# One table of 785 steps in another order, and two small PSUM banks named apart

## The chip, the cores and the metric

The kernel runs on one core of one Trainium2 chip. The metric is the device time of one launch in microseconds. The kernel before takes 190.54 us in the median of three runs (190.48, 190.54 and 190.9).

## What is computed

Attention with a window of 96 keys and 8 global keys, for 4 batches of 8 heads (768 tokens, 64 features a head), followed by a mixture of experts in which every expert reads 4 slots that are softmax mixtures of all tokens:

```python
def _attn_ref(q, k, v, n_global, n_local):
    scores = scale * np.matmul(q, k.transpose(0, 1, 3, 2))
    ...
    scores = np.where(keep, scores + bias, -1000000000.0)
    ...
    a = np.exp(scores - np.max(scores, axis=-1, keepdims=True))
    a = a / (np.sum(a, axis=-1, keepdims=True) + 1e-09)
    return np.matmul(a, v)

def _moe_ref(x, phi, w1, w2):
    logits = x @ phi                      # 3072 tokens, 32 slots
    ...
    slot_input = d.T @ x                  # d: softmax over the tokens
    ...
    slot_out[e] = np.maximum(slot_input[e] @ w1[e], 0.0) @ w2[e]   # 8 experts, hidden size 1024
    ...
    return c @ slot_out                   # c: softmax over the slots
```

## The kernel before

**Attention units.** The work of attention is cut into 16 units u (a batch and a pair of heads). For each unit, TensorE makes the scores in three parts (`scores`, L601) into two PSUM buffers. DVE adds the bias table and keeps a running maximum (`biased`, L610, three a unit). TensorE turns the maximum (`max_t`, L617), DVE reduces it (`max_n`, L622). ACT takes the exponential of each head i (`exponential`, L627) and rounds it to f16 (`w_hi`, L630). What the rounding leaves is made in three parts for each head, on POOL (`w_lo`) or on DVE (`w_lo_dve`), both recorded under L637. The values are split in the same way: the high half on ACT (`v_hi_act`, L575) or on POOL (`v_hi`, L572), the low half on DVE (`v_lo`, L579). TensorE multiplies 39 small tiles a head (`values`, L655; the last unit goes in halves, `valh`, L708). DVE then takes the sums, their reciprocals and the product out of PSUM (`ev_sums` L667, `ev_recs` L672, `ev_mul` L676). The product is turned (`tr`, L738) and copied (`tr_copy` on ACT, L744; `tr_copy_dve` on DVE, L749), and makes the logits (`logits`, L770). At the end of each batch (units 3, 7, 11, 15) follow `logits_all` (L787), `strip_max`, `strip_exp` (L811), `by_token` (L826), its copies, `dispatch` (L849) and `dispatch_sum` (L860, L866); `strip_sum` (L819, L821) adds up a denominator that is read only near the end.

**Experts.** Behind unit 15 the steps `ld_...` finish the slot inputs, `hid` (L115) is the first matrix product of the experts, `proj` (L149) the second, in two halves of the columns; `so` (L208, L209) scales a half, `cmb` (L1094) mixes it back to tokens, `cev` on ACT (L1100) and `cev_dve` on DVE (L1103) copy it out of PSUM, and `put` (L1107) sends 0.52 MB of output, 12 times. `check` (L1121 to L1132) and `flag` (L1137) decide whether a general path must run instead.

**Loads.** All loads are issued by SP, one after the other: `load_qk` (L457, 0.85 MB a unit, two buffers `raw0` and `raw1`), `load_v` (L460, 0.46 MB a unit, two halves of `vt`), and the weights (L438), 32 pieces of 1.05 MB. Pieces 0 to 9 have tiles of their own (`wp0` to `wp9`) and are loaded during attention (`piece`); `extra` loads parts of later pieces into space that attention leaves unused. `free` loads the rest of such a piece as soon as a buffer of attention is done, and `load` loads pieces 23 to 31, most of them over pieces that `hid` has used. An instruction of SP that waits holds back all that stand behind it.

**The order.** Everything stands in one list, `ORDER`, that is walked once (`for name, u, *args in ORDER: steps[name](u, *args)`). Each step appends its instructions to their engines, and each engine runs its own in that order. No scheduler moves anything later. Each of the steps of TensorE that needs a small PSUM bank takes one from `Banks.tile`; during attention there are two such banks, both under the tag `m` of a pool with two buffers.

## Time and profile before

| what | value |
|---|---|
| median of three runs | 190.54 us |
| span of the profiled execution (no other time is given for it) | 190.8 us |
| busy: PE, DVE, ACT, POOL | 170.4, 144.1, 127.0, 96.9 us |
| moved by DMA | 61.34 MB, mean 321 GB/s |
| first `biased`, end of the last `w_lo_dve` | 7.98 us, 126.6 us |
| first `hid`, last copy of `cmb` | 136.30 us, 181.0 us |

Busy shares are averages over the two very different stretches, attention up to some 128 us and the experts behind it. The page's chain of waits is empty for this execution, so its path has to be read from the waits of each engine, from the timeline and from tables of short stretches.

### The profile page before, as it was taken

To read this page: it belongs to the slowest core of one execution; us is meant where nothing else is said; L and a number is where in the kernel's file an instruction comes from. 1 tells how busy PE (TensorE), PEld (TensorE's weight loads), DVE (VectorE), ACT (ScalarE), POOL (GpSimd) and SP (SyncE) were. 2 spreads that over 40 slices of the span, in tenths; PEclk is the share of its full clock that TensorE was granted. 3 is DMA by queue.
4 is the path that set the end of the run, shared out by engine and by line. 5 is a ranking of instruction groups with operands and counts; after the bars stand their busy time and mean duration, and the time that the engine had idled before them with its cause. 6 is when DMAs were issued, how large, how long until landed. Compare 5 with 4: busy or idle time off the path is not lost.

```text
span 190.8 us, 6334 instructions
## 1 busy us (share of the span) xinstructions
PE 170.4 (89%) x2629; PEld 127.6 (67%) x2629; DVE 144.1 (75%) x353; ACT 127.0 (67%) x165; POOL 96.9 (51%) x121
## 2 busy tenths in 40 slices
PE   8898999999997988899999999897999999998600
PEld 2454988889895787689878887784622566875400
DVE  4899999999988999879999999996850413535600
ACT  3068799899999598698999999964204352632600
POOL 7506687788679776679696897500004040000000
PEclk9999999999999999999999999999999999999975
DMA  3998999989999999619519977899999999977992
GB/s 108 411 405 294 339 411 414 386 344 364 367 406 401 380 332 356 228 32 334 174 41 352 336 267 225 279 413 349 364 423 425 404 417 410 399 258 265 324 330 89
DMA packets 18609, 61.34 MB, mean 321 GB/s; under 512 B 1680, under 2 KB 8976, under 8 KB 16144
## 3 DMA queue, kind: packets, MB, share of 16 engines
q1 hardware_dynamic: 18432, 60.89, 85.4%
q8 instruction: 22, 0.36, 0.7%
q14 instruction: 11, 0.09, 0.1%
q10 hardware_dynamic: 144, 0.00, 0.0%
HBM read 54.59 MB, written 6.29 MB: 319 GB/s over the span
## 4 chain that ended last, share of the span: by engine, by line


## 5 line engine op out<-in xcount | busy, mean ns | idle before, releaser
L637 POOL TENSOR_TENSOR ph<-tb,ph 128x432 f16<-128x432 f32 x79 | 82.3, 1074 | 23.5 <-ACT ph L630 23.5
L601 PE MATMUL sc<-raw 64*128 64x216 f32 (+2 forms) x448 | 44.9, 337 | 3.1 <-DMA raw<-in_qk_dram 2.0
L627 ACT ACTIVATE tb<-tb,nb 128x1296 f32<-128x1296 f32 x32 | 43.7, 1374 | 2.0 <-DVE nb L622 1.9
L630 ACT CAST ph<-tb 128x1296 f16<-128x1296 f32 x32 | 40.6, 1272 | 5.2 <-PE x L655 4.6
L601 PEld LDWEIGHTS sc<-raw 64*128 64x128 f32 x448 | 37.0, 186 | 10.2 <-issue 3.3
L655 PEld LDWEIGHTS <-ph 128*128 128x128 f16 x1170 | 38.8, 97 | 2.9 <-issue 2.1
L655 PE MATMUL x<-v,ph 128*128 128x65 f16 (+1 forms) x1170 | 40.4, 193 | 0.0
L579 DVE SCALAR_TENSOR_TENSOR v<-vt,v 128x896 f16<-128x896 f32 x16 | 19.8, 1237 | 1.0 <-POOL v L572 1.0
L186 POOL TENSOR_TENSOR wp<-lnat,wp 120x448 f32<-120x448 f32 x4 | 4.5, 1150 | 29.0 <-ACT wp L181 29.0
L610 DVE CUSTOM_DVE_ANT_1 tb<-sc,tt,mx 128x864 f32<-128x864 f32 x16 | 17.7, 1108 | 0.7 <-DVE tt L296 0.2
L738 PE MATMUL m<-ident,xn 120*128 120x120 f32 x112 | 16.7, 275 | 1.4 <-DVE xmax L676 1.2
L575 ACT ACTIVATE v<-vt 128x896 f16<-128x896 f32 x12 | 11.4, 949 | 7.9 <-DMA vt<-in_v_dram 7.9
L676 DVE CUSTOM_DVE_ANT_1 xn<-x,rc 120x896 f32<-120x896 f32 x15 | 16.3, 1087 | 0.4
L738 PEld LDWEIGHTS m<-ident,xn 120*128 120x128 f32 x112 | 11.5, 141 | 4.1 <-issue 2.8
L637 DVE TENSOR_TENSOR ph<-tb,ph 128x432 f16<-128x432 f32 x17 | 11.4, 690 | 0.0
L115 PE MATMUL hp<-wp,sl 128*32 128x512 f32 x80 | 10.5, 593 | 0.0
L1100 ACT COPY xta<-m 128x512 f32<-128x512 f32 x7 | 4.0, 587 | 8.6 <-PE m L1094 8.5
L610 DVE CUSTOM_DVE_ANT_1 tb<-sc,xta,mx 128x864 f32<-128x864 f32 x8 | 8.9, 1112 | 0.5 <-DVE mx L610 0.2
L610 DVE CUSTOM_DVE_ANT_1 tb<-sc,xtt,mx 128x864 f32<-128x864 f32 x8 | 8.9, 1116 | 0.4 <-DVE mx L610 0.4
L610 DVE CUSTOM_DVE_ANT_1 tb<-sc,tt 128x864 f32<-128x864 f32 x8 | 8.4, 1050 | 0.2
L1103 DVE COPY tt<-m 128x512 f32<-128x512 f32 x5 | 3.4, 690 | 6.4 <-PE m L1094 6.4
L149 PE MATMUL o<-wp,wp 128*32 128x256 f32 x96 | 7.6, 380 | 0.0
(206 smaller groups left out, 283.6 us busy)
## 6 DMA issues: line engine op xcount, KB each, us to landing
wp<-in_w_dram SPq DMA_DIRECT2D x14, 1024.0 KB, 10.1
raw<-in_qk_dram SPq DMA_DIRECT2D x15, 832.0 KB, 6.7
vt<-in_v_dram SPq DMA_DIRECT2D x16, 448.0 KB, 6.7
wp<-in_w_dram SPq DMA_DIRECT2D x4, 512.0 KB, 12.7
raw<-in_w_dram SPq DMA_DIRECT2D x4, 512.0 KB, 13.7
out_dram<-xtt SPq DMA_DIRECT2D x4, 512.0 KB, 3.3
out_dram<-xta SPq DMA_DIRECT2D x4, 512.0 KB, 6.6
out_dram<-tt SPq DMA_DIRECT2D x4, 512.0 KB, 5.7
```

What stands on the lines that cost most here:

```text
L115: nc.tensor.matmul(out=hp[n][32 * s:32 * s + 32, :], lhsT=slv(a, c, s), rhs=w1(e, c // 2)[:, (c % 2) * DF + 512 * n:(c % 2) * DF + 512 * n ...
L149: nc.tensor.matmul(out=o[32 * s:32 * s + 32, 0:w], lhsT=ht[:, c, 32 * s:32 * s + 32], rhs=w2(4 * a + s, half)[:, c0 + c * w:c0 + c * w + w ...
L575: nc.scalar.activation(out=vhi[u % 2][:, :, :, 0:D], in_=vraw[u % 2], func=AF.Copy, scale=V_SC)
L579: nc.vector.scalar_tensor_tensor(out=vlo[k].rearrange("p j i d -> p (j i) d"), in0=vraw[k].rearrange("p j i d -> p (j i) d"), scalar=V_SC, ...
L601: nc.tensor.matmul(out=z[:, i, at:at + n], lhsT=r_[r, KCOL[j]:KCOL[j] + KR], rhs=r_[r, KW + KB * j:KW + KB * j + n], start=True, stop=True)
L610: nc.vector.tensor_tensor_reduce(out=tb(u)[:, :, BW * k:BW * k + BW], in0=sc[(3 * u + k) % 2][:, :, 0:BW], in1=table.unit(u % NP, k), scal ...
L627: nc.scalar.activation(out=t, in_=t, func=AF.Exp, bias=nbs[u], scale=T_SC)
L630: nc.scalar.copy(out=blocks(phi_[i])[:, :, 0:QW], in_=tb(u)[:, i].rearrange("p (s c) -> p s c", c=QW))
L637: (engine or nc.gpsimd).tensor_tensor(out=blocks(plo_[i])[:, c, 0:QW], in0=tb(u)[:, i].rearrange("p (s c) -> p s c", c=QW)[:, c], in1=bloc ...
L655: nc.tensor.matmul(out=xf[:, at(t, i):at(t, i) + d], lhsT=w[:, c:c + P], rhs=vv[:, j, i, 0:d], start=z in first, stop=(z == len(ops) - 1), ...
L676: nc.vector.tensor_tensor_reduce(out=xnb[(u // 2) % 3][:, p].rearrange("p t (i d) -> p (t i) d", i=2), in0=xv[:, :, 0:D], in1=rcs.pop(u).u ...
L738: nc.tensor.transpose(out=m[:, at:at + KB], in_=xnb[(u // 2) % 3][:, p % 2, t, :], identity=ident[0:KB, 0:KB])
```

## The change

The list holds the same 785 steps, each as often as before, with the same arguments; they stand in another order from the first step to the last. The steps that go to DVE and those that go to POOL stay the same, so no instruction is added or removed. As the pieces of weights take their places by the order of `free`, some pieces of the experts lie in other tiles (piece 11 in `tb1` and no longer in `raw1`, for example). The two small banks, so far two buffers of one tag, become two tags `m0` and `m1`, which are taken in turn.

```diff
-ORDER = [('load_qk0', 0), ('hint', 0, 'Pool'), ('keys', 0), ('extra', 0), ('scores', 0, 0), ('load_qk', 0), ('table_even', 0),
+ORDER = [('keys', 0), ('table_even', 0), ('load_v', 0), ('warm', 0, 1), ('load_qk0', 0), ('load_qk', 0), ('scores', 0, 0),
...
-    psm = banks.enter_context(tc.tile_pool(name="psm", bufs=2, space=PSUM))
+    psm = banks.enter_context(tc.tile_pool(name="psm", bufs=1, space=PSUM))
...
-        tags = ("m", "m")
+        tags = ("m0", "m1")
...
-            return (psm if tag == "m" else self.pool).tile([P, 512], F32, name=name, tag=tag)
+            return (psm if tag[0] == "m" else self.pool).tile([P, 512], F32, name=name, tag=tag)
...
-            left.next(("l2", "l3", "m", "m", "l0", "l1"))
+            left.next(("l2", "l3", "m0", "m1", "l0", "l1"))
```

**Place 1: SP, the loads of units 6 to 11.** `vt` is the load of a unit's values, `raw0` and `raw1` those of an even and an odd unit's queries and keys, `wp5` to `wp8` pieces of weights. Before, from the loads of values 7 and 6 to those of unit 11's queries:

```order
L460 DMA vt_102<-in_v_dram 128x896 x2
L438 DMA wp6_86<-in_w1_dram 128x2048
L457 DMA raw1_91<-in_qk_dram 128x1664
L438 DMA wp7_87<-in_w1_dram 128x2048
L460 DMA vt_102<-in_v_dram 128x896
L438 DMA wp8_88<-in_w1_dram 128x2048
L457 DMA raw0_90<-in_qk_dram 128x1664
L460 DMA vt_102<-in_v_dram 128x896
L457 DMA raw1_91<-in_qk_dram 128x1664
```

Now, from the piece ahead of values 6 to unit 11's queries:

```order
L438 DMA wp5_85<-in_w1_dram 128x2048
L460 DMA vt_102<-in_v_dram 128x896
L457 DMA raw1_91<-in_qk_dram 128x1664
L460 DMA vt_102<-in_v_dram 128x896
L438 DMA wp7_87<-in_w1_dram 128x2048
L457 DMA raw0_90<-in_qk_dram 128x1664
L460 DMA vt_102<-in_v_dram 128x896 x2
L457 DMA raw1_91<-in_qk_dram 128x1664
```

Ahead of unit 10's queries (the last `raw0` of both lists) nine pieces stood in the whole queue, and six do now (9, 8, 0, 1, 5 and 7, in that order); pieces 2, 4, 6 and 3 follow later. Values 6 stand ahead of values 7.

**Place 2: DVE, unit 5's sums.** `rsall` is `ev_sums`, `v` is `v_lo` of unit 6, `ph` is a `w_lo_dve`, `state` (L819) is `strip_sum` of the first batch. Before, from the first `biased` of unit 8 to `ev_mul` of unit 5:

```order
L610 ISA tb_98,mx<-sc_172,tt 128x2x432
L610 ISA mx 128x1
L667 TENSOR_TENSOR rsall<-x,eps 120x14
L579 SCALAR_TENSOR_TENSOR v_101<-vt,v_101 128x896
L672 RECIPROCAL rc<-rsall 120x2x7
L622 ISA mxd,nb<-m,shift 128x128
L622 ISA nb 128x1
L819 COPY state<-al 128x1
L676 ISA xn_106,xmax<-x,rc 120x896
```

Now, the same stretch:

```order
L610 ISA tb_98,mx<-sc_172,tt 128x2x432
L610 ISA mx 128x1
L804 TENSOR_SCALAR state<-al 128x1
L622 ISA mxd,nb<-m,shift 128x128
L622 ISA nb 128x1
L610 ISA tb_98,mx<-sc_173,tt,mx 128x2x432
L610 ISA mx 128x1
L637 TENSOR_TENSOR ph_99<-tb_96,ph_99 128x2x216
L667 TENSOR_TENSOR rsall<-x,eps 120x14
L672 RECIPROCAL rc<-rsall 120x2x7
L579 SCALAR_TENSOR_TENSOR v_101<-vt,v_101 128x896
L676 ISA xn_106,xmax<-x,rc 120x896
```

A `biased`, a `max_n` and a `w_lo_dve` now stand ahead of the sums and of `v_lo`; `strip_sum` is gone from here and stands two units later, behind the reciprocals of unit 7.

**Place 3: DVE, the end.** `so` is the second half's scaling, `fl` is `check`, `flag` the decision, L1103 the copies of `cmb`. Before:

```order
L1131 TENSOR_REDUCE fl<-fl 128x1
L1132 TENSOR_SCALAR fl<-fl 128x1
L208 TENSOR_SCALAR so<-o,sgz 128x256
L209 SCALAR_TENSOR_TENSOR so<-o,sgz,so 128x256
L1103 COPY tt<-m 128x512
L1103 COPY xtt<-m 128x512
L1103 COPY xta<-m 128x512
L1137 TENSOR_SCALAR flag<-m 1x1
L1103 COPY tt<-m 128x512 x2
```

Now:

```order
L1103 COPY v_101<-m 128x512 x2
L208 TENSOR_SCALAR so<-o,sgz 128x256
L209 SCALAR_TENSOR_TENSOR so<-o,sgz,so 128x256
L1121 TENSOR_REDUCE fl<-fl 120x1
L1122 TENSOR_SCALAR fl<-fl 120x1
L1121 TENSOR_REDUCE fl<-rsall 120x1
L1122 TENSOR_SCALAR fl<-fl 120x1
L1121 TENSOR_REDUCE fl<-rsall 48x1
L1122 TENSOR_SCALAR fl<-fl 48x1
```

The check stood ahead of `so` and stands behind it now, ahead of DVE's five last copies.

## Rows read from the trace of the kernel before

**Rows 1.** The page: busy time by engine, and DMA's busy tenths in 40 slices.
```profile
PE 170.4 (89%) x2629; PEld 127.6 (67%) x2629; DVE 144.1 (75%) x353; ACT 127.0 (67%) x165; POOL 96.9 (51%) x121
...
DMA  3998999989999999619519977899999999977992
```

**Rows 2.** Table of stretches, 56 to 88 us: us, busy of PE, PEld, DVE, ACT, POOL, clock, DMA share, GB/s.
```profile
56.00:64.00 8.00, 6.84 (x123) 5.42 (x121) 6.62 (x15) 5.91 (x9) 7.03 (x7) 1.00 0.98 389
64.00:72.00 8.00, 7.23 (x123) 6.36 (x123) 7.82 (x18) 7.38 (x8) 5.57 (x5) 1.00 0.94 360
72.00:80.00 8.00, 6.70 (x122) 5.54 (x121) 7.67 (x17) 5.41 (x9) 6.11 (x6) 1.00 0.86 320
80.00:88.00 8.00, 8.00 (x153) 7.17 (x151) 6.21 (x13) 7.98 (x9) 5.93 (x6) 1.00 0.35 106
```

**Rows 3.** DVE's groups, 7.9 to 126.7 us: busy us, mean ns, idle ahead and releaser.
```profile
L579 DVE SCALAR_TENSOR_TENSOR v<-vt,v 128x896 f16<-128x896 f32 x16 | 19.8, 1237 | 1.0 <-POOL v L572 1.0
...
L637 DVE TENSOR_TENSOR ph<-tb,ph 128x432 f16<-128x432 f32 x17 | 11.4, 690 | 0.0
...
L667 DVE TENSOR_TENSOR rsall<-x,eps 120x14 f32<-120x14 f32 x15 | 2.5, 168 | 2.4 <-PE x L655 2.4
```

**Rows 4.** Waits of the whole span: who waited for whom, us in total, times, longest.
```profile
DVE rsall L667 <- PE x L655: 2.4, 4, 1.6
...
PE sc L601 <- DMA raw<-in_qk_dram: 2.0, 2, 1.3
...
PE m L849 <- DVE state L819: 1.2, 1, 1.2
```

**Rows 5.** Timeline of SP, POOL, DVE and PE: start us, us, instruction, idle ahead.
```profile
49.33 0.80 SPq L460 DMA_DIRECT2D vt<-in_v_dram  x2
...
56.99 0.94 POOL L572 TENSOR_SCALAR v<-vt 128x896 f16<-128x896 f32 x1 [0.96 <-DMA vt<-in_v_dram]
...
57.97 1.89 DVE L579 SCALAR_TENSOR_TENSOR v<-vt,v 128x896 f16<-128x896 f32 x1 [1.00 <-POOL v L572]
...
82.02 0.17 DVE L667 TENSOR_TENSOR rsall<-x,eps 120x14 f32<-120x14 f32 x1 [1.58 <-PE x L655]
...
77.22 1.00 PE L601 MATMUL sc<-raw 64*128 64x216 f32 x8 [1.30 <-DMA raw<-in_qk_dram]
```

**Rows 6.** Single lines and tiles: durations in ns, min/median/max.
```profile
L579 DVE SCALAR_TENSOR_TENSOR v<-vt,v x16: 1078/1086/1933, 15.0 to 121.3; 128x896 f16<-128x896 f32 x16
...
L637 DVE TENSOR_TENSOR ph<-tb,ph x17: 596/606/1010, 28.5 to 126.0; 128x432 f16<-128x432 f32 x17
...
L637 POOL TENSOR_TENSOR ph<-tb,ph x79: 997/1012/1861, 15.9 to 122.4; 128x432 f16<-128x432 f32 x79
```

**Rows 7.** Table of stretches again, at attention's end and in the experts' part.
```profile
112.00:116.00 4.00, 3.71 (x72) 3.07 (x70) 3.95 (x11) 4.00 (x8) 3.92 (x5) 1.00 0.67 183
...
140.00:144.00 4.00, 4.00 (x40) 1.17 (x36) 1.09 (x5) 0.61 (x2) 0.00 (x0) 1.00 1.01 428
...
171.00:172.00 1.00, 1.00 (x24) 0.62 (x20) 0.90 (x6) 0.26 (x1) 0.00 (x0) 1.00 0.11 39
...
186.00:187.00 1.00, 0.00 (x0) 0.00 (x0) 0.00 (x0) 0.00 (x0) 0.00 (x0) 0.50 1.00 333
```

**Rows 8.** Timeline: first `biased`, last run of `w_lo_dve`, first `hid`, `check`, last `put`.
```profile
7.98 1.06 DVE L610 CUSTOM_DVE_ANT_1 tb<-sc,tt 128x864 f32<-128x864 f32 x1
...
123.84 2.77 DVE L637 TENSOR_TENSOR ph<-tb,ph 128x432 f16<-128x432 f32 x5
...
136.30 0.62 PE L115 MATMUL hp<-wp,sl 128*32 128x512 f32 x2
...
171.44 0.15 DVE L1121 TENSOR_REDUCE fl<-fl 120x1 f32<-120x2 f32 x1
...
173.24 0.15 DVE L1132 TENSOR_SCALAR fl<-fl 128x1 f32<-128x1 f32 x1
...
181.78 1.28 SPq L1107 DMA_DIRECT2D out_dram<-tt  x1
```

More of the change, by code (lines that the diff above doesn't have):

```diff
@@ L485, in blocks @@
         return w[:, 0:6 * PB].rearrange("p (s c) -> p s c", c=PB)
-    wp = psm.tile([P, 512], F32, name="wp", tag="m")
+    wp = psm.tile([P, 512], F32, name="wp", tag="m0")
     busy_in = nc.const_aps.tensor(1.0, [P, 512], BF16)
@@ L567, in pair_of_banks @@
             return [left.wide.tile([P, 512], F32, name="hp", tag=f"y{n}") for n in range(2)]
-        left.next(("l2", "l3", "m", "m"))
+        left.next(("l2", "l3", "m0", "m1"))
         return [left.pool.tile([P, 512], F32, name="hp", tag=f"l{n}") for n in range(2)]
```

2 lines of the change are left out of this document (1 added, 1 removed).

## The prediction, made blind

> **What bounds the kernel now.** The page comes first [rows 1]: PE is busy for 170.4 us, DVE for 144.1, but these are averages over two stretches. DMA's tenths show 9 nearly everywhere, a valley in slices 16 to 20 (76 to 100 us), and 9 again from slice 26 (124 us) nearly up to the end. So I read the two stretches apart.
>
> In attention I look for the engine that never rests. DVE's groups between 7.9 and 126.7 us [rows 3] show only a few microseconds of idle time, most of it in two places: the sums out of PSUM waited 2.4 us for `values` in four units, and one `v_lo` waited 1.0 us. PE and ACT have little more room, so a stall of one of them soon reaches DVE. The table of 8 us stretches [rows 2] shows where it happened: between 56 and 88 us DVE was busy for 6.62, 7.82, 7.67 and 6.21 us, which leaves 3.7 us of idle time in 32. In the first three of these stretches DMA was at 0.98, 0.94 and 0.86 of its capacity; the loads of the next units shared it with pieces of weights that nobody needs before `hid` starts, at 136.30 us [rows 8].
>
> The list of waits [rows 4] ties the two together. PE waited 2.0 us for queries and keys, and `dispatch` 1.2 us for a small DVE instruction (L819). In the timeline [rows 5] the values of unit 6 are issued from 49.33 us on, behind those of unit 7; POOL waits 0.96 us for them, until 56.99, and `v_lo` 1.00 us for POOL. PE gets unit 11's queries at 77.22, 1.30 us late, and DVE stands for 1.58 us, until 82.02, before the sums of unit 8.
>
> Behind attention DMA stays at 1.0 of its capacity, moving 428 GB/s at 140 us, while PE shows no idle time either [rows 7]. There loads and matrix products keep pace with each other. The output leaves at some 333 GB/s, and DMA still works at 186 us, 4 us behind SP's last issue at 181.78 [rows 7, 8].
>
> **The change, part by part.** Nothing is added or removed, so the busy time of each engine stays as it is; only waits, and durations that depend on a neighbour, can change.
>
> *Values of unit 6.* Counted through the list, 16.7 MB stand ahead of them in place of 18.8: a piece less (1.05 MB), three extras less (0.61) and the values of unit 7 (0.46), 2.1 MB in all. At 389 GB/s [rows 2] this is 5.4 us of transfers. It is far more than the 0.96 us that POOL waited [rows 5], so this wait should go, and with it the 1.0 us of DVE. Bounds: no gain, if POOL's step comes late for another reason; a gain of 1.8 us, if the 0.8 us by which this `v_lo` was stretched (1.89 us against a median of 1.086, [rows 5, 6]) go too. I take 1.0, the wait itself.
>
> *Queries of units 10 and 11.* Ahead of unit 10's stand 19.5 MB in place of 23.7: three pieces (3.15 MB), values 8 (0.46) and three extras (0.61) have moved behind. That is 4.2 MB, 10.8 us at 389 GB/s. PE's two waits of together 2.0 us should go, and with them the sums' wait of 1.58 us. Bounds: 0 and 2.0 us, PE's own sum. I take 1.6. The pieces moved behind fall into the valley, where DMA stood at 0.35 [rows 2]: 4.2 MB in some 20 us are no load there, and nothing waits for them. This is the cover of the move; if the pieces of the valley were late, `hid` would wait for them at 136 us, more than 30 us later.
>
> *`strip_sum`.* `dispatch` of the first batch no longer has L819 ahead of it. PE's 1.2 us [rows 4] lay in the same 56 to 64 us as the wait for unit 6's values, so I count nothing more: 0 to 1.2 us.
>
> *Two-input DVE steps beside POOL.* Most `v_lo` take 1.09 us, but the mean is 1.237, which is 16 × 0.15 = 2.4 us above the median in all, three steps of some 0.8 us [rows 3, 6]. The 17 `w_lo_dve` lose 17 × 0.084 = 1.4 us in the same way (mean 690 ns, median 606). POOL's own steps reach 1.861 us against 1.012. So the two engines do hold each other up, and the gain of an order that avoids it all would be 3.8 us of DVE. The loss of an order in which every `v_lo` is hit would be 13 × 0.8 = 10.4 us. In the new list `v_lo` still stands between parts of `w_lo`, so I can't see from the order which of them meet. I take 0, the value nearest to today's three of sixteen.
>
> [...]
>
> *The start.* Values 0 now go ahead of unit 0's queries, 0.46 MB, 1.2 us at the same rate; the first `biased` starts at 7.98 us [rows 8], when DVE has built its table. 0, at worst +1.
>
> *The experts.* The pieces are issued in another order, but the bytes are the same, and the large buffers now come ahead of the small ones. If attention ends earlier, `free` is issued earlier by as much, so loads and products move together. At the end, `check` has moved behind the second `so`: 13 small instructions from 171.44 to 173.4 us [rows 8], about 2 us on DVE, before its five last copies. ACT copies meanwhile, and the outputs have a backlog on DMA; at most I expect 1.5 us more, at best 1.9 less, since the second-half loads could end before the first `put` and fill the hole at 171 us, where DMA stood at 0.11 [rows 7]. I take 0.
>
> **The sum.** 190.8 (span) − 1.0 − 1.6 = 188.2 us. The median of the runs is 0.3 below this execution, so the time predicted is **187.9 us**, 1.4% faster.
>
> **The rivals.**
>
> *More than that (faster).* DVE loses 1.6 us less of the 3.8 to its meetings with POOL, and `dispatch` counts for 1.0: another 2.6 us, 185.3. For it speaks that PE, ACT and DVE lost time in the same stretch. Against it speaks that each of the three has so little room that the next bound is near.
>
> *The gain is lost behind attention (no change).* DMA has no free time from 124 us on [rows 1], and the first `free` needs unit 13's tables. If the loads, not the end of attention, set the time, 2.6 us gained by 82 us come back as a wait of `proj` for its last pieces: 190.5 us. Against it: between 112 and 116 us DMA was at 0.67 [rows 7], so an earlier `free` finds room.
>
> *DVE and POOL meet more often (slower).* The new order packs `v_lo` of units 2, 9, 11 and 13 between other parts of `w_lo` than before. If eight of sixteen are stretched in place of three, that is 5 × 0.85 = 4.3 us more, and 190.5 − 2.6 + 4.3 = 192.2. It decides from three more stretched steps on, 2.6 us; below that the change is still a gain. [...]
>
> *New waits for `values` (slower).* In units 1, 7, 10 and 11 `ev_sums` stands one or two `biased` earlier in DVE's list than before. If each of the four waits as unit 8 did, half of 1.58 us on the mean, 3.2 us come on top: 191.1. DVE would stand with `biased` queued behind, and PE would wait for its score buffers. Against it: `values` has moved forward in PE's list in unit 7 too.
>
> **How the numbers follow.** I give the forecast 0.48, the larger gain 0.15, the loss behind attention 0.12, more meetings 0.13 and new waits 0.12. Two parts in a thousand, 0.4 us, are about what a measurement of this kernel can tell from no change. The gain lost behind attention and the slower edge of the forecast make "same" 0.10; the first two cases with their spread make "faster" 0.65; the rest is "slower", 0.25. The forecast's own range is 186.4 to 189.8 (all of the two waits and the `strip_sum`, or half of the waits with a worse end). For eight in ten I go down to 185.0, the larger gain with its spread, and up to 191.6, which takes in new waits and half of the case with more meetings.
>
> **What would show it.** Right: no wait of POOL for `vt`, none of PE for `raw` between 60 and 80 us, no wait above 1 us of L667 for `values`; the last `w_lo_dve` ends at some 124 us in place of 126.6, `hid` starts at 133.7 in place of 136.3 [rows 8], and DMA stands near 0.8 in the old valley. [...] If attention ends where it did, my first two terms were not on the path.

## The result, and the profile after

The changed kernel takes 191.9 us in the median of 20 runs (190.68 to 194.65), the kernel before 190.95 us beside it (20 runs, 189.89 to 192.19). The ratio is 1.0056, with a 95% interval of 1.0029 to 1.0083: slower by half a percent, where 1.4% faster was forecast. A ratio leaves out runs more than 1.5% above the fastest of their kernel, the medians quoted do not; for a kernel with much scatter the two can differ.

The runs of the changed kernel also lie further apart, 4.0 us against 2.3. One more thing has to be known to read the two profiles. In every execution that has both numbers, the time is 1.8 to 2.0 us more than the span. So the traced execution of before, with its span of 190.8 us, took some 192.6 us, more than any of the 20 runs; the traced execution after, span 188.9 us, took 190.68 us and was the fastest of its 20. The two profiles show the change better than it is.

Of the page after, busy time, PE's clock and DMA's tenths (before: [rows 1]):

```profile
PE 169.7 (90%) x2629; PEld 125.8 (67%) x2629; DVE 141.4 (75%) x353; ACT 126.6 (67%) x165; POOL 95.4 (50%) x121
...
PEclk9999999999999999999999999999999999999975
DMA  3998997987998769998989749999999999589993
```

The valley of slices 16 to 20 is gone, as the change moves pieces there; but a new dip (5 and 8) stands in slices 34 and 35, 160 to 170 us. The table of stretches, 56 to 88 us (before: [rows 2]):

```profile
56.00:64.00 8.00, 8.00 (x164) 6.55 (x161) 7.96 (x19) 7.31 (x11) 6.12 (x6) 1.00 0.91 339
64.00:72.00 8.00, 8.00 (x140) 6.84 (x137) 7.14 (x18) 7.86 (x9) 5.83 (x6) 1.00 0.64 212
72.00:80.00 8.00, 8.00 (x139) 6.64 (x140) 7.55 (x16) 6.90 (x10) 6.91 (x8) 1.00 1.00 395
80.00:88.00 8.00, 8.00 (x140) 6.67 (x142) 7.83 (x24) 7.23 (x11) 7.66 (x8) 1.00 0.85 321
```

PE has no idle time in these 32 us, and DVE 1.5 us in place of 3.7. DVE's groups from 7.9 to 123.5 us and the waits (before: [rows 3, 4]):

```profile
L579 DVE SCALAR_TENSOR_TENSOR v<-vt,v 128x896 f16<-128x896 f32 x16 | 18.7, 1168 | 0.0
...
L637 DVE TENSOR_TENSOR ph<-tb,ph 128x432 f16<-128x432 f32 x17 | 10.9, 668 | 0.0
```

```profile
PE sc L601 <- DMA raw<-in_qk_dram: 1.3, 1, 1.3
DVE rsall L667 <- PE x L655: 1.0, 2, 0.6
...
PEld o L149 <- DMA wp<-in_w_dram: 2.0, 1, 2.0
PE o L149 <- DMA wp<-in_w_dram: 1.8, 1, 1.8
```

No row names POOL's wait for `vt`, and the sums wait 1.0 us in place of 2.4. PE's one wait for `raw` is at the start, before the first scores. New are two waits of `proj` for weights. Last, the timeline (before: [rows 8]), with the second `so` (L208, L209) and the check behind it:

```profile
8.15 1.06 DVE L610 CUSTOM_DVE_ANT_1 tb<-sc,tt 128x864 f32<-128x864 f32 x1
...
120.79 2.68 DVE L637 TENSOR_TENSOR ph<-tb,ph 128x432 f16<-128x432 f32 x5
...
133.08 1.49 PE L115 MATMUL hp<-wp,sl 128*32 128x512 f32 x12
...
172.88 0.48 DVE L209 SCALAR_TENSOR_TENSOR so<-o,sgz,so 128x256 fp32r<-128x256 f32 x1
...
175.08 0.15 DVE L1132 TENSOR_SCALAR fl<-fl 128x1 f32<-128x1 f32 x1
...
180.59 1.47 SPq L1107 DMA_DIRECT2D out_dram<-tt  x1
```

The last `w_lo_dve` ends at 123.47 (126.61 before), `hid` starts at 133.08 (136.30), the last `put` is issued at 180.59 (181.78). The signs that I had named for being right are there; the old valley, for which I had named 0.8, stands at 0.78 to 1.01 in stretches of 4 us. A sign of the rival in which the gain is lost behind attention is there as well: `hid` is early and `proj` waits for weights. The span is 1.9 us shorter than that of before, where 2.6 were forecast, so this one execution would nearly have confirmed the prediction. The runs do not.

### The profile page after: what moved, and what is told of

It is laid out like the page before. It is cut to its first block, busy times and chain, and to the rows that moved or that the text cites. A ratio compares the mean times of both kernels' runs of the same rounds, so it can differ in the third digit from the quotient of the medians.

```text
span 188.9 us, 6327 instructions
## 1 busy us (share of the span) xinstructions
PE 169.7 (90%) x2629; PEld 125.8 (67%) x2629; DVE 141.4 (75%) x353; ACT 126.6 (67%) x165; POOL 95.4 (50%) x121
## 4 chain that ended last, share of the span: by engine, by line
## 5 line engine op out<-in xcount | busy, mean ns | idle before, releaser
L637 POOL TENSOR_TENSOR ph<-tb,ph 128x432 f16<-128x432 f32 x79 | 81.1, 1060 | 28.1 <-ACT ph L630 26.0
L601 PE MATMUL sc<-raw 64*128 64x216 f32 (+2 forms) x448 | 45.7, 340 | 1.6 <-DMA raw<-in_qk_dram 1.3
L579 DVE SCALAR_TENSOR_TENSOR v<-vt,v 128x896 f16<-128x896 f32 x16 | 18.7, 1168 | 0.0
L637 DVE TENSOR_TENSOR ph<-tb,ph 128x432 f16<-128x432 f32 x17 | 10.9, 668 | 0.0
L115 PEld LDWEIGHTS hp<-wp,sl 128*32 128x32 f32 x80 | 2.9, 110 | 6.6 <-issue 6.3
L115 PE MATMUL hp<-raw,sl 128*32 128x512 f32 x16 | 7.2, 592 | 0.0
```

Source lines behind the costliest of these rows:

```text
L115: nc.tensor.matmul(out=hp[n][32 * s:32 * s + 32, :], lhsT=slv(a, c, s), rhs=w1(e, c // 2)[:, (c % 2) * DF + 512 * n:(c % 2) * DF + 512 * n ...
L579: nc.vector.scalar_tensor_tensor(out=vlo[k].rearrange("p j i d -> p (j i) d"), in0=vraw[k].rearrange("p j i d -> p (j i) d"), scalar=V_SC, ...
L601: nc.tensor.matmul(out=z[:, i, at:at + n], lhsT=r_[r, KCOL[j]:KCOL[j] + KR], rhs=r_[r, KW + KB * j:KW + KB * j + n], start=True, stop=True)
L637: (engine or nc.gpsimd).tensor_tensor(out=blocks(plo_[i])[:, c, 0:QW], in0=tb(u)[:, i].rearrange("p (s c) -> p s c", c=QW)[:, c], in1=bloc ...
```

## Experiments

All of them are compared with the same kernel before. Medians are in us, ratios against before with their 95% interval. The moves are in `ORDER` only, unless the diff shows something else; "..." leaves out steps.

### Second traces, and the two halves exchanged

No edit: both kernels once more.

> The kernel before once more, to have a second execution of it in the trace. The first one spans 190.8 us; by the 1.78 us that lie around the span in every run, it took some 192.6 us, more than any of the 20 runs of before (189.89 to 192.19). Theory S (the trace that I argued from was an untypical one): this execution spans about 189.2 us, the last w_lo_dve ends near 125.0 us in place of 126.60, PE's waits for queries and keys at 60 to 80 us are under 1 us in all. Rival T (it was typical, and the change's tail gives the gain back): the last w_lo_dve ends within 0.5 us of 126.60, and the span differs by under 1 us.

> The changed kernel once more. Its first execution in the trace spans 188.9 us (190.68 us of time, the fastest of 20 runs, which reach to 194.65). Theory S: a typical execution spans 190.1 us, with the last w_lo_dve at 124.5 to 125.5 us in place of 123.47, so that attention is no faster than before's. Rival T: the last w_lo_dve ends at 123.5 within 0.5 us again, and what differs between executions lies behind hid, at 133 us and later.

Measured: before again 190.38 (ratio 0.9967, 0.9932 to 1.0003), the changed kernel again 191.41 (1.0036, 1.0003 to 1.0069). The first ratio compares a kernel with itself, so a comparison can be 0.3% off. For before, rival T came true: the second traced execution, a time of 192.45 and the longest of its 12 runs, was as long as the first, and `w_lo_dve` ends at 126.81. For the changed kernel both theories fell: the second execution (192.94) ends attention 3.5 us later than its first, at 129.10 against 125.57 by the last `ev_mul`, and all of it arises in attention: 1.08 us ahead of the first `biased`, the rest at 9 us, at 29 to 35 us and at 83 to 86 us. So the difference between executions does not lie behind `hid`. In the second execution of before the waits that I had priced stand elsewhere, as DVE's timeline shows (the first: [rows 5]):

```profile
59.16 1.88 DVE L579 SCALAR_TENSOR_TENSOR v<-vt,v 128x896 f16<-128x896 f32 x1 [2.24 <-POOL v L572]
...
82.23 0.17 DVE L667 TENSOR_TENSOR rsall<-x,eps 120x14 f32<-120x14 f32 x1
```

Then the new attention with the old tail, and the reverse:

```diff
-[changed order up to ('strip_max', 15)] + [changed order behind it]
+[changed order up to ('strip_max', 15)] + [what is left, in the order of before]
```

```diff
-[order of before up to ('strip_max', 15)] + [order of before behind it]
+[order of before up to ('strip_max', 15)] + [what is left, in the changed order]
```

> The changed order up to the strip_max of unit 15, and from there what is left in the order of before. Theory T (the new tail loses it): attention ends at 123.5 us as in the changed kernel, and the time is 188.5 us, 2.4 below before's 190.95. Rival V (the new attention is what scatters and loses): 191.9 us like the changed kernel, with runs 3 us or more apart. Theory S: within 0.5 us of before.

> The order of before up to the strip_max of unit 15, and from there what is left in the changed order. Theory T: slower than before by 1.5 us or more, 192.5 to 194. Rival V: like before, 191.0 us, with runs under 2.5 us apart. Theory S: 191 to 192, the tail costing half a microsecond to one.

Measured: 196.28 (1.028, 1.0234 to 1.0327) and 192.06 (1.0041, 1.0011 to 1.0072). The first does not tell the theories apart, since the splice makes a wait that neither kernel has. Timeline of PE and table of stretches of the first:

```profile
137.61 1.07 PE L115 MATMUL hp<-wp,sl 128*32 128x512 f32 x2 [3.14 <-DVE sl L99]
```

```profile
136.00:140.00 4.00, 2.39 (x12) 0.59 (x16) 3.25 (x10) 0.00 (x0) 0.00 (x0) 0.55 1.04 382
140.00:144.00 4.00, 4.00 (x28) 1.03 (x24) 0.00 (x0) 0.00 (x0) 0.00 (x0) 0.60 0.67 282
```

`hid` waits 3.14 us for the slot inputs, and then runs at a lower granted clock (0.55 and 0.60 on the mean over these stretches, 1.00 over 128 to 136 and 144 to 148 us) up to 144 us. The second one suggests that the new tail costs some 0.4%. In its traced execution `hid` starts 8.2 us behind the last `ev_mul`, against 7.5 to 7.6 in the traced kernels that are not spliced, so a part of it may come from the splice. It stays a hint.

### The start

In the changed order the values of unit 0 go first. The small load `nraw`, 16 bytes a partition, which ACT issues at 0.73 us and which DVE needs for the bias table, then comes later. DVE's timeline of before, and of the changed kernel's first and second execution:

```profile
4.67 0.19 DVE L1013 CAST nf<-nraw 128x4 f32<-128x4 int32 x1 [1.35 <-DMA nraw<-in_n_dram]
4.90 0.33 DVE L273 TENSOR_SCALAR xn<-xn,nf 128x216 f32<-128x216 f32 x1
```

```profile
5.26 0.17 DVE L1013 CAST nf<-nraw 128x4 f32<-128x4 int32 x1 [1.94 <-DMA nraw<-in_n_dram]
5.47 0.38 DVE L273 TENSOR_SCALAR xn<-xn,nf 128x216 f32<-128x216 f32 x1
```

```profile
5.83 0.21 DVE L1013 CAST nf<-nraw 128x4 f32<-128x4 int32 x1 [2.51 <-DMA nraw<-in_n_dram]
6.07 0.86 DVE L273 TENSOR_SCALAR xn<-xn,nf 128x216 f32<-128x216 f32 x1
...
9.23 1.06 DVE L610 CUSTOM_DVE_ANT_1 tb<-sc,tt 128x864 f32<-128x864 f32 x1
```

Against the first execution of before `nraw` is 0.6 to 1.2 us late. Over all traced executions DVE starts on it at 4.67 to 5.28 us where queries are SP's first load, and at 5.26 to 5.88 where the values are. In the third fence L273 takes 0.86 us in place of 0.33; it now runs beside POOL's setup work, whose L511 starts at 6.05. The four experiments take the move back, make it in the kernel before, and part its two effects:

```diff
-('load_v', 0), ('warm', 0, 1), ('load_qk0', 0), ('load_qk', 0), ..., ('load_qk', 1),
+('warm', 0, 1), ('load_qk0', 0), ('load_qk', 0), ..., ('load_qk', 1), ('load_v', 0),
```

> The changed kernel with one load moved: the values of unit 0 go behind the queries and keys of units 0 and 1, as in the kernel before, not ahead of them. Theory start (my price of 0 for this move is wrong: the first biased starts at 8.15, 9.23 and 9.14 us in three executions with the changed start, at 7.98, 8.00 and 7.97 in three with the old one): the first biased starts at 8.0 us, the small load nraw lands at 4.65 us in place of 5.2 to 5.8, no PE instruction in 6 to 10 us runs at the lower clock, and the time falls by 0.9 us against after_again, to 190.5. Rival (the tail is limited by its loads, so a start that is 1 us earlier is given back): the first biased at 8.0, the time 191.2 to 191.5 as in after_again.

> start_back once more, beside the same runs of before: if its 189.87 stands, its ratio to before is 0.990 to 0.997 again. If it was a draw of the scatter that the changed order has: 191.0 to 191.7, as start_values2 and start_spread, ratio 1.000 or more.

Measured: 189.87 (0.9935, 0.9900 to 0.9970), and in the repetition 190.48 (0.9980, 0.9943 to 1.0016). The two differ as much as such intervals allow; their mean, 0.9958, is 0.9% below the mean of the changed kernel's two comparisons (1.0046), some 1.7 us. The repetition lies between its two expectations: the gain over before is smaller than it first looked, that over the changed kernel stands.

The reverse, in the order of before:

```diff
-('load_qk0', 0), ('hint', 0, 'Pool'), ..., ('load_qk', 1), ('load_v', 0), ...
+('load_v', 0), ('load_qk0', 0), ('hint', 0, 'Pool'), ..., ('load_qk', 1), ...
```

> The kernel before, with one load moved as the change moves it: the values of unit 0 go ahead of everything, the queries and keys of unit 0 behind them. Theory start: nraw lands at 5.2 to 5.8 us in place of 4.65, the first biased starts at 8.5 to 9.2 us, and the time is 191.8 to 192.3, 1.0 to 1.5 above before. Rival (the new order of attention alone is sensitive to a late start): the first biased is late in the same way, and the time within 0.4 us of before's 190.8, since the loads of units 6 to 11 set the pace there.

Measured: 192.5 (1.0087, 1.0053 to 1.0122): 0.9%, 1.7 us again. PE's timeline, and the stretch 8 to 12 us in this kernel and, below it, in before:

```profile
7.32 1.73 PE L601 MATMUL sc<-raw 64*128 64x216 f32 x8 [2.20 <-DMA raw<-in_qk_dram]
```

```profile
8.00:12.00 4.00, 4.00 (x23) 2.40 (x23) 3.00 (x7) 0.00 (x0) 0.00 (x0) 0.64 1.02 395
```

```profile
8.00:12.00 4.00, 3.42 (x30) 1.95 (x26) 3.70 (x10) 1.46 (x2) 0.00 (x0) 1.00 1.05 401
```

PE stood for 2.20 us before its first scores, and then worked at a mean granted clock of 0.64, where before has 1.00. So there are two candidates for the price: the late table, and PE's wait with the lower clock behind it. One kernel, made from start_back, has the table's delay alone; one, made from the changed kernel, puts the values between unit 0's two loads:

```diff
-        nc.vector.tensor_scalar(out=self.t, in0=self.rel, scalar1=nlo, ...)
+        for _ in range(4):
+            nc.vector.tensor_scalar(out=self.t, in0=self.rel, scalar1=nlo, ...)
```

> start_back, in which the first instruction of DVE on nraw's numbers is made four times over in place of once, with the same operands, so that the bias table is ready some 0.85 us later while every load stands as in start_back. If the delay of the table is what costs: the first biased starts at 8.85 us, and the time is 0.85 above start_back's 189.87, 190.7. If a shift also breaks up the order's timing of DVE and POOL: 191.3 or more. If the loads set the pace, and the table has room: 189.9.

```diff
-('load_v', 0), ('warm', 0, 1), ('load_qk0', 0), ('load_qk', 0),
+('warm', 0, 1), ('load_qk0', 0), ('load_v', 0), ('load_qk', 0),
```

> The changed kernel, with the values of unit 0 between the first and the second part of unit 0's queries and keys. nraw and the first scores should come as early as before (4.65 and 6 us), the second scores 1.1 us later. If it is the late nraw, and with it the bias table, that costs: 189.9 us, as start_back. If it is PE's wait for queries and keys, and the lower clock after it: 190.9 to 191.9, as the changed kernel, with the wait now ahead of the second scores.

Measured: late_table 192.8 (1.0016, 0.9974 to 1.0058), with runs from 190.14 to 195.12; v0_second 190.95 (1.0019, 0.9983 to 1.0054). In late_table the first `biased` starts at 9.24, 1.23 us later than in start_back; its fastest run is 1.0 and 1.4 us above the fastest runs of the two start_back, its median 2.3 and 2.9 us above theirs. By the ratios, which differ from the medians here because the runs scatter so much, the delay costs 0.4 to 0.8%. No load was moved, so a late table alone can cost a good part of what the whole move costs. PE's timeline of late_table, and the stretch 8 to 12 us:

```profile
10.36 1.06 PE L602 MATMUL sc<-raw 64*128 64x216 f32 x4 [2.53 <-DVE mx L611]
```

```profile
8.00:12.00 4.00, 1.64 (x12) 1.62 (x12) 3.56 (x10) 0.95 (x1) 0.00 (x0) 0.80 1.01 415
```

The table comes late, so PE stands 2.53 us for the score buffers that DVE has not freed, and its granted clock is lower as well: 0.80 over 8 to 12 us and 0.77 over 12 to 16, where start_back has 1.00 in both. The two candidates are thus not independent: here the lower clock came with the late table alone. v0_second did not part them. `nraw` was no earlier than in the changed kernel's first execution (DVE starts on it at 5.28), the first `biased` started at 8.12 with a clock of 1.00 over 8 to 12 us, and the median lies some 0.8 us above the mean of the two start_back. So the price is shown for the move as a whole; how it divides is open.

The size of SP's first load goes with it in sign: where it is the queries, 2,368 bytes a partition (296 KB), DVE starts on `nraw` at 4.67 to 5.28 us, and where it is the values, 3,584 bytes a partition (448 KB), at 5.26 to 5.88. But it does not do so strictly: in v0_second the queries go first and the values behind them, and `nraw` is as late (5.28) as in the changed kernel's first execution (5.26). No run here varies the size of that load alone, so what holds `nraw` back is not shown.

### The check and the two banks

```diff
-('so', 1), ('cev', 0, 9), ('check', 0),
+('check', 0), ('so', 1), ('cev', 0, 9),
```

> The changed kernel with check moved back ahead of the second so. Theory check (my price of 0 for it is wrong: the stretch from the end of the second so to the last copy of cmb is 5.93, 5.93 and 5.76 us in three executions with the old tail, 6.71, 7.53 and 7.54 with the new one): that stretch is 5.9 us, the last output lands 0.8 to 1.6 us earlier after the second so, and the time is 190.4. Rival (the outputs have a backlog on DMA that hides the copies): the stretch is 5.9 us, and the time 191.2 to 191.5.

> Both moves together: values of unit 0 behind the first queries and keys, check ahead of the second so. If both theories hold: 189.5 us, 0.6% below before's 190.71 of the last comparison and faster than both kernels. If only one holds: 190.4. If the loads of the tail hold everything back: 191.2 to 191.5.

Measured: check_back 192.1 (1.0055, 1.0011 to 1.0099), both_back 189.97 (0.9962, 0.9927 to 0.9998). The check's place moves nothing: the changed kernel stays at 1.0055, and with the start mended at 0.996. The stretch from the second `so` to the last copy did not come down to 5.9 us either (6.49 and 7.13), so the check's place does not lengthen it, the new order of `cmb` and its copies may, and the expectation fell in both its parts. That the time does not follow it fits the rival, a backlog of outputs on DMA: from the end of the second `so` to the end of the span lie 15.5 to 16.2 us in the traced executions with the new tail, 15.7 to 15.8 with the old one.

The trace of check_back is also a second look at the dip of DMA after 160 us. It is an execution of 189.04 us whose attention ended at the same time as in the first one of the changed kernel (125.74 and 125.57). First the changed kernel, then check_back:

```profile
160.00:164.00 4.00, 2.22 (x26) 1.41 (x25) 1.56 (x3) 1.04 (x2) 0.00 (x0) 1.00 0.79 319
164.00:168.00 4.00, 4.00 (x50) 2.72 (x54) 1.06 (x2) 1.69 (x4) 0.00 (x0) 1.00 0.57 188
```

```profile
160.00:164.00 4.00, 4.00 (x52) 2.78 (x54) 2.41 (x4) 2.46 (x6) 0.00 (x0) 1.00 0.81 326
164.00:168.00 4.00, 4.00 (x64) 2.55 (x60) 1.99 (x7) 1.33 (x3) 0.00 (x0) 1.00 0.90 306
```

PE lost 1.8 us there in one execution and none in the other. By the trace's landing times, one piece of weights landed 4.04 us behind the piece ahead of it in the first, 2.50 us in the other, and all behind it are 2.3 us later. So the new waits of `proj` in the profile after belong to that execution, not to the order: no other traced execution of the changed order shows more than 0.2 us of them. The first execution of before has such a step too, a piece that landed 4.05 us behind the one ahead of it, and 2.50 in the second.

```diff
-    psm = banks.enter_context(tc.tile_pool(name="psm", bufs=2, space=PSUM))
...
-        tags = ("m", "m")
+    psm = banks.enter_context(tc.tile_pool(name="psm", bufs=1, space=PSUM))
...
+        tags = ("m0", "m1")
```

> The order of before, with the two small banks as two tags that are taken in turn. My step counted nothing for them: within 0.3% of before. Rival (the strict alternation makes a step wait for a bank whose neighbour is free): 0.5 to 1.5 us slower, with waits of PE for a bank's reader that before does not show.

Measured: 190.91 (0.9986, 0.9959 to 1.0013). The banks' names are worth nothing by themselves. This execution (191.07) is also a more usual one of the order of before: POOL's wait for `vt` was 1.5 us, PE's for `raw` 0.6, and attention ended at 127.51 in place of 128.68.

### The loads of units 6, 10 and 11 alone

```diff
-('piece', 5), ('load_v', 7), ('load_v', 6), ('piece', 6), ('load_qk', 9), ('piece', 7), ('load_v', 8), ('piece', 8),
-('load_qk', 10), ('load_v', 9), ('load_qk', 11), ('piece', 9), ('load_v', 10),
+('load_v', 6), ('piece', 5), ('load_v', 7), ('load_qk', 9), ('load_v', 8),
+('load_qk', 10), ('load_v', 9), ('load_qk', 11), ('piece', 6), ('piece', 7), ('piece', 8), ('piece', 9), ('load_v', 10),
```

> The kernel before, with nothing but four loads of SP moved, those of my first two terms: the values of unit 6 go ahead of piece 5 (so ahead of those of unit 7), and pieces 6, 7 and 8 behind the queries of unit 11. If the two terms are right as such: no wait of POOL for vt at 58 us, none of PE for queries and keys at 60 to 80 us, and 188.2 us, 2.6 below before's 190.8. If they were right for the traced execution alone, which took 1.8 us more than the median: 189.8. Rival (the next bound takes it, or the loads behind attention give it back): the waits are gone and the time is within 0.3 us of before.

Measured: 197.54 (1.0355, 1.0311 to 1.0400), 6.5 us slower, which no theory had. POOL's timeline, DVE's, and the stretch 92 to 96 us:

```profile
85.24 0.94 POOL L572 TENSOR_SCALAR v<-vt 128x896 f16<-128x896 f32 x1 [6.88 <-DMA vt<-in_v_dram]
```

```profile
93.59 1.06 DVE L610 CUSTOM_DVE_ANT_1 tb<-sc,tt 128x864 f32<-128x864 f32 x1 [4.92 <-PE sc L601]
```

```profile
92.00:96.00 4.00, 4.00 (x29) 3.31 (x28) 2.40 (x4) 1.32 (x3) 3.70 (x4) 0.50 0.00 0
```

Up to 82 us this execution is 2.50 us ahead of before's, nearly the 2.6 forecast. Then the values of unit 10, which stand behind four pieces now, come 6.88 us late, `biased` of DVE waits 4.92 us, and PE's granted clock is 0.50 over 88 to 92 and over 92 to 96 us. The stretch from unit 11 to unit 15 takes 39.3 us in place of 30.1. So the queue was right for the loads that I looked at, and wrong for those behind them. Two more kernels spread the pieces:

```diff
-... ('load_qk', 11), ('piece', 9), ('load_v', 10), ('load_qk', 12), ('load_qk', 13), ('load_v', 11), ('load_v', 12), ...
+... ('load_qk', 11), ('piece', 6), ('load_v', 10), ('load_qk', 12), ('piece', 7), ('piece', 8), ('load_qk', 13), ('load_v', 11), ('piece', 9), ('load_v', 12), ...
```

> The kernel before, with the loads of loads_alone, in which the pieces that move behind are spread: piece 6 behind the queries of unit 11, then the values of unit 10 and the queries of unit 12, then pieces 7 and 8, and piece 9 behind the values of unit 11. In loads_alone DVE was 2.50 us ahead of before at 82 us, and lost 9 us by 91 us to values of unit 10 that came 6.9 us late behind four pieces. If that queue is the whole of it: no wait of POOL for vt above 1 us, the stretch from the last biased of unit 7 to that of unit 11 takes some 27.7 us in place of 29.6 to 30.9, and the time is 188.3 to 189.5. If the stretch behind 82 us has another bound, or the experts' loads give it back: within 0.4 us of before.

```diff
-... ('load_qk', 11), ('piece', 6), ('load_v', 10), ('load_qk', 12), ('piece', 7), ('piece', 8), ('load_qk', 13), ('load_v', 11), ('piece', 9), ('load_v', 12), ('load_qk', 14), ...
+... ('load_qk', 11), ('load_v', 10), ('load_qk', 12), ('piece', 6), ('load_qk', 13), ('load_v', 11), ('load_v', 12), ('piece', 7), ('piece', 8), ('load_qk', 14), ('piece', 9), ...
```

> loads_spread, with the pieces further back: the values of unit 10 and the queries of unit 12 directly behind the queries of unit 11, then piece 6, the queries of unit 13, the values of units 11 and 12, pieces 7 and 8, the queries of unit 14, piece 9. If the pieces' places are what gave back 1.7 us between 94 and 103 us: no wait of POOL for vt above 1 us, the stretch from unit 11 to unit 15 at 30.1 us in place of 31.7, and a median 1 us below loads_spread's 190.06, 189.0. If the stretch has another bound (meetings of DVE and POOL, the engines' own work): 189.8 to 190.3.

Measured: loads_spread 190.06 (0.9949, 0.9912 to 0.9985), loads_spread2 189.56 (0.9933, 0.9901 to 0.9965): 1.27 us below before, and the lowest median here, though the intervals of loads_spread and start_back overlap with its own. POOL's timeline in loads_spread; then 56 to 80 us in loads_spread2:

```profile
93.70 0.94 POOL L572 TENSOR_SCALAR v<-vt 128x896 f16<-128x896 f32 x1 [4.12 <-DMA vt<-in_v_dram]
```

```profile
56.00:64.00 8.00, 8.00 (x145) 6.20 (x142) 7.62 (x18) 7.04 (x9) 6.59 (x7) 1.00 0.69 247
64.00:72.00 8.00, 8.00 (x144) 7.36 (x140) 7.82 (x20) 7.64 (x10) 6.17 (x7) 1.00 0.56 178
72.00:80.00 8.00, 8.00 (x156) 7.06 (x153) 7.85 (x19) 7.69 (x10) 6.32 (x8) 1.00 0.74 287
```

PE is never idle there, and DMA has room, at a busy share of 0.56 to 0.74. Both kernels are 4.0 us ahead of the first execution of before at 82 us, and 2.9 us ahead of the more usual one of banks_only. So the earlier loads are worth up to there what I had forecast; what is behind takes more than half of it back. loads_spread gives part of it back to values of unit 12 that come 4.12 us late behind pieces. loads_spread2 has not lost it by 104 us; it loses 0.9 us by 113 us and 0.5 more by 120. At the first of these ACT stands for 1.27 us and starts at 107.56 with `v_hi` of unit 14, whose values landed at 107.48, 8.6 us behind their issue (the trace names PE's scores as the releaser); the same load took 5.4 us in before. Each time, a load further back in the queue takes over.

### What else scatters in the changed order

```diff
-('load_qk', 3), ..., ('piece', 8), ..., ('load_qk', 4), ('load_v', 2),
+('load_qk', 3), ..., ('load_v', 2), ('piece', 8), ..., ('load_qk', 4),
```

> start_back, with the values of unit 2 ahead of piece 8 too. In the changed order the stretch from the first biased to the last of unit 7 takes 46.15 to 46.28 us in three executions and 47.26 to 47.49 in four; in the latter ACT waits 0.9 to 1.6 us at 27 us for values. If that wait makes the difference: the stretch is 46.2 us, and the median 189.0, 0.9 below start_back's 189.87. If the stretch's two lengths come from DVE meeting POOL: 189.87, within 0.3.

```diff
-('piece', 2), ('load_v', 10), ('load_qk', 12), ..., ('piece', 4), ..., ('piece', 6), ..., ('load_qk', 13), ('load_v', 11), ('load_v', 12),
+('load_v', 10), ('load_qk', 12), ('piece', 2), ..., ('load_qk', 13), ('piece', 4), ('load_v', 11), ('load_v', 12), ('piece', 6),
```

> start_values2, with three pieces moved back in the queue: piece 2 behind the queries of unit 12, piece 4 behind those of unit 13, piece 6 behind the values of unit 12. If late queries of units 12 and 13 are what makes the changed order scatter behind 72 us: no wait of PE for raw behind 72 us, the stretch from unit 11 to unit 15 at 30.2 us, runs less than 2.5 us apart, and a median of 188.5 to 189.0. If meetings of DVE and POOL make the scatter: no change against start_values2, with runs 3 us or more apart.

Measured: 191.7 (1.0001, 0.9964 to 1.0039) and 190.87 (1.0019, 0.9988 to 1.0050). The wait at 27 us went, and the stretch up to unit 7 took 46.35 and 46.26 us, as expected; the time did not fall, and both ratios lie above those of the two start_back. Nor did start_spread calm the runs much (190.33 to 192.72): PE still waited 1.26 us for `raw` at 97 us in the traced one. Both expectations fell. What can be shown is where the executions differ. From DVE's timeline, all in us: start of the first `biased`, then from there to the end of the last `biased` of unit 7, on to that of unit 11, on to that of unit 15, and the end of the last `ev_mul`:

| execution (its time) | first | to 7 | to 11 | to 15 | end |
|---|---|---|---|---|---|
| before (some 192.6) | 7.98 | 47.45 | 30.60 | 30.06 | 128.68 |
| before again (192.45) | 8.00 | 47.33 | 30.92 | 30.04 | 128.88 |
| banks_only (191.07) | 8.03 | 47.33 | 29.59 | 30.05 | 127.51 |
| before_new_start (192.29) | 9.16 | 48.49 | 28.46 | 30.06 | 128.76 |
| loads_spread2 (189.94) | 7.91 | 47.33 | 26.82 | 31.15 | 126.33 |
| changed (190.68) | 8.15 | 46.16 | 28.68 | 30.21 | 125.57 |
| changed again (192.94) | 9.23 | 47.26 | 28.51 | 31.72 | 129.10 |
| check_back (189.04) | 8.48 | 46.15 | 28.52 | 30.22 | 125.74 |
| start_back (192.58) | 8.01 | 47.44 | 31.13 | 30.20 | 129.16 |
| start_back again (190.54) | 8.06 | 47.72 | 28.49 | 30.30 | 126.94 |
| both_back (190.93) | 8.00 | 47.47 | 28.87 | 30.20 | 126.91 |
| start_values2 (190.88) | 8.00 | 46.35 | 30.50 | 30.20 | 127.43 |
| start_spread (190.75) | 7.97 | 46.26 | 28.63 | 31.68 | 126.92 |
| v0_second (192.11) | 8.12 | 47.49 | 28.50 | 31.76 | 128.25 |

The order of before varies in one column, that of units 8 to 11. The changed order takes one of two lengths in each of three, 0.9 to 2.6 us apart, and ahead of each long one a load is late. Up to unit 7, ACT waits 0.9 to 1.9 us for unit 2's values in the five long ones, 0.2 us at most in the short ones. Up to unit 11, ACT waits 2.08 and 1.06 us for unit 8's values in the two long ones (start_back, start_values2), 0.43 us at most in the others. Up to unit 15, PE waits 0.30, 0.72 and 1.26 us for queries in the three long ones, and not behind 80 us in the others. The first of the three was tested: start_values2 and start_spread load unit 2's values sooner, and the stretch is short. The other two are read from traces alone.

Here is the second column in start_back (192.58 us, the longest of its 12 runs) and, below it, in its repetition:

```profile
68.79 0.95 ACT L575 ACTIVATE v<-vt 128x896 f16<-128x896 f32 x1 [2.08 <-DMA vt<-in_v_dram]
...
73.97 1.01 POOL L637 TENSOR_TENSOR ph<-tb,ph 128x432 f16<-128x432 f32 x1 [3.55 <-ACT ph L630]
...
81.01 1.02 PE L655 MATMUL x<-v,ph 128*128 128x65 f16 x28 [1.34 <-POOL ph L637]
...
82.08 0.17 DVE L667 TENSOR_TENSOR rsall<-x,eps 120x14 f32<-120x14 f32 x1 [1.97 <-PE x L655]
```

```profile
67.31 0.95 ACT L575 ACTIVATE v<-vt 128x896 f16<-128x896 f32 x1 [0.29 <-DMA vt<-in_v_dram]
...
77.77 1.83 DVE L579 SCALAR_TENSOR_TENSOR v<-vt,v 128x896 f16<-128x896 f32 x1
...
80.49 0.16 DVE L667 TENSOR_TENSOR rsall<-x,eps 120x14 f32<-120x14 f32 x1
```

The values come 1.5 us later, POOL starts its `w_lo` 1.5 us later behind ACT, `values` waits 1.34 us for POOL, and DVE's sums 1.97 us for `values`. A `v_lo` of 1.84 us beside POOL's `w_lo` stands there too, at 77.29 us; but the repetition has the same one (1.83 us) and no wait behind it, so this meeting is not what makes the stretch long. By the trace's landing times the lateness begins one load earlier: unit 10's queries landed 5.03 us behind the piece ahead of them in start_back, 3.34 us in the repetition, although they were issued 0.3 us sooner. In the second execution of the changed kernel unit 12's queries landed 4.85 us behind the load ahead of them, 2.89 in the first; they come 0.30 us late at 83 us, and at 88 us a `v_lo` is stretched to 1.78 us. So executions of one kernel differ by single transfers that take 1.5 to 2 us longer. Why a transfer does so in one execution and not in the next is not settled.

The first two columns also hold the price of a late start: before_new_start and late_table (first `biased` at 9.24, then 48.42, 28.87 and 30.21) start 1.2 us later than before and start_back, and take 0.7 to 1.2 us more up to unit 7. In the changed order the move has a gain beside it. With the values of unit 0 in front, ACT waits 0.2 to 0.9 us for unit 2's values (the changed kernel's two executions, check_back, new_att_old_tail); in the four that load unit 0's values later and nothing else sooner (both start_back, both_back, v0_second) it waits 1.4 to 1.9 us. So the price of the move is seen in the medians and in the changed kernel's second execution, not in its first.

## Why the prediction was wrong

**The start** is the step that failed: "0, at worst +1". The move costs 0.9%, some 1.7 us, in either order. I had compared the values' 1.2 us with the time at which DVE has its table, and took the table for independent of the loads; but it is made from `nraw`, which is a load too, and whose wait of 1.35 us stands in DVE's timeline of before. What the runs show in its place is a first `biased` 0.2 to 1.2 us later and, behind PE's waits of 1.87 and 2.20 us, a granted clock of 0.64 on the mean over 8 to 12 us (1.00 in before). Without that move the changed order is 0.2 to 0.65% faster than before, on the side that was forecast; but start_values2 and start_spread, which move further loads, came out at 1.0001 and 1.0019, so this gain is no larger than what such a move can take away.

**The base** was the second error. "190.8 (span) ... the median of the runs is 0.3 below this execution" set a span against times. The execution was some 1.7 us above the median, and a good part of the waits that I meant to save was that excess: the stretch of units 8 to 11 took 30.6 us in it, 29.6 in a more usual one, and takes 28.5 to 28.9 in the changed order when nothing else happens. So the two terms, −2.6 us, were −1.0 against the usual execution and −1.9 against the one that I read. That there are two of them was wrong as well: in the second execution of before `v_lo` stood for 2.24 us in place of 1.00, and the sums behind for 0.08 in place of 1.58. It is one lag of DMA, and a late wait is covered by an earlier one.

**The cover** of the moved pieces was named wrongly: "nothing waits for them". Nothing waits for the pieces, but the values of unit 10, and later those of units 12 and 14, stand behind them on SP; in loads_alone this cost 9 us, PE's time at a clock of 0.50 included. In the changed order itself the pieces stand better, but loads are late there too: values by up to 2.08 us at 69 us, queries by 0.30 to 1.26 us behind 80 us, in some executions and not in others.

**DVE beside POOL**, counted at 0, was right in size: in the two traced executions of the changed kernel two and four `v_lo` are above 1.4 us (three before), and together the sixteen lose 1.3 and 2.2 us over the median (2.4 before). The rival with more meetings fell. At the start, too, single steps are longer where both engines work: POOL's L511 and DVE's table instructions meet at 6.06 us, and in one execution POOL takes 0.99 us for 0.29, in the other DVE's L273 takes 0.86 for 0.33. L273 reads one tensor, not two, so a DVE step that is longer beside POOL need not be one with two inputs, the only ones that the prediction counts. What makes such a step longer, no run shows.

**The experts and the check**, 0 with bounds of −1.9 and +1.5: right for the check, and nearly so for the rest. From the last `ev_mul` to the end of the span lie 61.4 to 63.3 us with the new tail, 61.7 to 62.1 with the old one, and old_att_new_tail puts the new tail's price at 0.4%, some 0.8 us at most, inside the bounds. The rival by which the loads give the gain back shows in one execution alone. **The `strip_sum`**, and with it the rest of place 2, was not tried by itself.

The sum with the measured terms: +1.7 us for the start, as before_new_start alone gives it, and 0.4% of gain, some −0.8, for all the rest (earlier loads, late ones behind them, the tail) give +0.9 us; measured were +0.56% and +0.36%, 1.1 and 0.7 us. Of the 3.6 us between the −2.6 forecast and the measured +1.0, about half is the start, and half that all the rest gained 0.8 us where 2.6 were forecast.

## What to carry to other kernels

Before costs are read from one trace, set its own time (not its span) beside the median of the runs: a stall that only a long execution has is no gain to be had. When a load is moved forward in a queue, ask of each load that it passes who waits for that one, and of every load behind the new place too; the tiny first loads count, if the first table is made from them. When two executions of one kernel differ, follow the delay back to the first load that is late, and look whether the suspect stands in the faster execution too.

## What was not expected of the hardware

- A load of 16 bytes a partition on ACT's queue, issued at 0.73 us each time, was usable by DVE at 4.67 to 5.28 us where SP's first load, at 0.74 us, was queries, and at 5.26 to 5.88 us where it was values.
- A piece of weights landed 2.50 us behind its predecessor in one execution, 4.04 us in another, with the same loads around it; DMA moved 405 GB/s at full share over 156 to 160 us, ahead of the late landing at 160.26 us. The same happened to queries (3.34 and 5.03 us). What held them is open.
- After PE's idle time of 2.20 us at the start (before_new_start) the granted clock was 0.64 on the mean over 8 to 12 us, and 0.64 after one of 1.87 us (the changed kernel's second execution); after one of 1.32 us (its first) it was 1.00. Between the two executions of the changed kernel, 0.55 us more of waiting thus went with 0.64 in place of 1.00.
